# Row sums in tiles of 32 columns, two unused products at the passage to attention, and score banks that lie on those of the projection

## The chip, the core and the metric

The kernel runs on one core of a Trainium2 chip. The core has five engines with instruction streams of their own: TensorE (PE, matrix products; its weight loads are listed as PEld), VectorE (DVE), ScalarE (ACT), GpSimd (POOL) and SyncE (SP, which here issues nearly all DMA transfers). [...] Each engine works through its own stream in order, so an instruction that waits holds up all that stand behind it on that engine. Data lie in SBUF (128 partitions) and in PSUM, where TensorE writes its products: eight banks of 128 partitions by 512 floats.

The metric is device time in microseconds (us). The time before is 2242.26 us, the median of 3 runs (2241.82 to 2245.19).

## The reference, cut to what matters

A transformer block on 2048 tokens of width 576, with all shifts, scales and gates computed from one conditioning row `c`:

```python
mod = (_silu(c) @ w_mod).reshape(1, 6, 1, -1)
sa, ca, ga, sb, cb, gb = (mod[:, i] for i in range(6))
h = _layernorm(x) * (1 + ca) + sa
# attention: 32 heads of width 18, one key head and one value head for all
q, k, v = h @ wq, h @ wk, h @ wv
p = softmax(q k^T * 18**-0.5)
x = x + ga * ((p v) @ wo)
h = _layernorm(x) * (1 + cb) + sb
# channel MLP, hidden width 4608; the layernorm stands inside it once more
x = x + gb * (gelu(_layernorm(h) @ w1 + b1) @ w2 + b2)
```

Everything is in float32. The six rows of `mod` are 576 wide. Rows 0 and 1 are needed at the start; rows 2 to 5 (`ga`, `sb`, `cb`, `gb`) only after attention.

## The kernel before, in words

The program has three stages, and the pool of PSUM tiles is closed and opened again between them (`open_ps`). A new pool hands out banks in the order in which its kinds of tiles are first asked for, and a tile that lies on a bank of the old pool waits for the last users of the old tile there.

**Stage 1** computes the first layernorm and the projections, in four blocks of 512 tokens and five chunks of columns each (`q_chunk`; its product is a tile psB). Here psA has banks 0 to 3 (two tiles of two banks), psC bank 4, psB banks 5 to 7. Already in stage 1 some row maxima of the scores of the first two head groups are computed: `smax_half` (called by `unit`) forms scores in two psA tiles with four products and VectorE reduces each tile (line 337). The last `unit` stands at the end of the last chunk (line 470).

`busy(n)` multiplies the identity with itself n times into a psB tile that nobody reads. It is called three times near the start of the program.

**Stage 2** is attention, in 32 steps called quads (4 heads by 512 tokens). Within a quad the order of the work is written out by hand as a string of tokens (`QUAD`, `QUADW`):

- S: one product of scores, keys by queries, into a psB tile (line 901), and its exponential by ScalarE (line 903) into a tile P. 64 of them in a quad.
- M, R: scores for the row maxima of the *next* quad into a psM tile (line 319), reduced by VectorE (lines 923 and 921). X: an additional difference product for them (line 911) that ScalarE clips (line 914).
- V1 to V4: P times values into psC (line 891), as four products that each write 32 rows of the output and use 32 columns of the array; the digit says how many times 128 columns of P they take. When a quad is through, ScalarE copies psC out (line 715).

S products wait for the maxima of their quad, which come as DMAs of a few rows (line 364). Before, stage 2 asks for psB first (banks 0 to 3), then psM (4 to 6), then psC (7).

After every fourth unit of V, `between` lets a generator, `fill`, take one step: at every odd block of keys. The first filler is `late_weights`. It loads rows 3, 2 and 5 of `w_mod` as tiles of 128 partitions (line 527), multiplies them with silu(c) and adds the five chunks up on GpSimd (`total`, lines 498 and 501). What is left is a sum over the 128 partitions, wanted in every partition: `bcast` multiplies by a 128x128 matrix of ones (`unity`) in two halves of 288 columns (line 521), and VectorE writes the result to its destination (line 522): `BC` for rows 3, 4, 5 and `gab` for row 2. Row 4 follows some steps later in the buffer that row 5 leaves free (line 92), as does `wo` in that of row 2 (line 540); `gab` is then multiplied into `wo` by GpSimd (line 550). These results are first needed several quads later.

**Stage 3** is the MLP, 36 passes over groups of hidden columns, in a Strassen-like form: products of operands `OP` with weights (line 1111), GELU, and a second product into psA (lines 1214 and 1248) which VectorE adds to XT (lines 1220 and 1285). The operands of the second half of the tokens are formed during pass 17 by `form`, from pieces R of `yr`; "=T4" is one subtraction of 128x1024 elements, "+T4" its high part by ScalarE (line 1023), "-T4" its low part (line 1025). `op_pieces(R, e2)` takes the engine for some of them: VectorE for the first half of the tokens, GpSimd for the second.

## Time and profile before

| | |
|---|---|
| median of 3 runs | 2242.26 us |
| the profiled execution, its own time | 2243.08 us |
| its span, first to last instruction | 2241.3 us |
| PE busy | 2212.7 us (99%) |
| DVE busy | 1940.8 us (87%) |
| ACT busy | 1645.1 us (73%) |
| POOL busy | 1524.7 us (68%) |
| mean granted TensorE clock | 0.998 |

In a row of the timeline the first number is the start in us from the start of the span, the second the duration, then engine, line, operation, output and inputs, shapes, how many instructions the row holds, and in square brackets how long the engine was idle before it and what ended that. In a row of stretches there follow, after the length of the stretch, the busy times of PE, PEld, DVE, ACT and POOL with their instructions, the granted TensorE clock, the busy share of the DMA engines, and GB/s. In a row of the chain of waits: start, duration, engine, output tile, line.

### The profile page before, as it was taken

The page shows a single profiled execution, that of the slowest core. Times are in us where ns is not written, and L with a number is a line of the kernel's source. Part 1 is how long each engine was busy: PE and PEld are TensorE (multiplying, and loading weights), DVE is VectorE, ACT ScalarE, POOL GpSimd, SP SyncE. Part 2 cuts the span into 40 slices and gives each one's busy share as a digit, 9 for nine tenths or more (in the row PEclk, how much of TensorE's full clock was granted, in tenths as well). Part 3 has the DMA queues.
Part 4 walks back from the last instruction along what each step waited for, and adds up shares of the span by engine and source line. Part 5 has one row for each costly group of instructions (what it writes and reads, how often), then busy time and mean ns, then how long its engine had stood idle before and what let it go on. Part 6 is the DMA issues. An engine that isn't in the chain of part 4 may idle for free.

```text
span 2241.3 us, 45781 instructions
## 1 busy us (share of the span) xinstructions
PE 2212.7 (99%) x16458; PEld 1442.2 (64%) x16458; DVE 1940.8 (87%) x3420; ACT 1645.1 (73%) x3145; POOL 1524.7 (68%) x1760
## 2 busy tenths in 40 slices
PE   7999999999999999999999999999999999999999
PEld 5644544444444544444444445888888888989898
DVE  7589999999999999999999982887888878888787
ACT  5569999999999999999999997444545544344443
POOL 6654356776877787777776300888888857877776
PEclk9999999999999999999999999999999999999999
DMA  6232034443433333343333101666666646676664
GB/s 229 85 129 75 15 114 138 133 142 110 138 121 126 121 122 115 124 139 115 117 127 127 49 13 48 194 177 179 180 178 176 190 122 181 182 213 191 177 183 125
DMA packets 182404, 303.79 MB, mean 136 GB/s; under 512 B 19243, under 2 KB 74923, under 8 KB 182177
## 3 DMA queue, kind: packets, MB, share of 16 engines
q1 hardware_dynamic: 182033, 300.72, 42.9%
q8 instruction: 130, 2.13, 0.4%
q14 instruction: 97, 0.79, 0.1%
q10 hardware_dynamic: 144, 0.15, 0.0%
HBM read 198.71 MB, written 93.19 MB: 130 GB/s over the span
## 4 chain that ended last, share of the span: by engine, by line
PE 86%; DVE 3%; ACT 3%; POOL 2%; issue 1%; DMA 0%; SPq 0%; POOLq 0%; ACTq 0%
PE psC L891 21%; PE psB L1111 18%; PE psA L1214 16%; PE psB L901 13%; PE psM L319 10%; PE psB L700 2%; ACT P L903 2%; PE psB L911 2%; DVE mx L923 1%; PE psA L1248 1%; PE psA L700 1%; DVE xc L921 0%; PE psB L155 0%; PE psB L357 0%; PE psB L248 0%
## 5 line engine op out<-in xcount | busy, mean ns | idle before, releaser
L903 ACT ACTIVATE P<-psB 128x512 f32<-128x512 f32 x2008 | 1043.8, 619 | 35.0 <-PE psM L319 12.3
L923 DVE TENSOR_REDUCE mx<-psM 128x1 f32<-128x512 f32 x1476 | 938.1, 683 | 37.5 <-PE psM L319 14.9
L319 PE MATMUL psM<-KS,qst 64*128 64x512 f32 x1722 | 601.2, 442 | 0.4 <-DVE mx L923 0.4
L901 PE MATMUL psB<-qst,KS 64*128 64x512 f32 x2008 | 585.1, 429 | 1.7 <-DVE mx L337 1.5
L891 PE MATMUL psC<-P,V 128*32 128x256 f32 (+3 forms) x6424 | 576.3, 448 | 0.5 <-ACT O L715 0.5
L901 PEld LDWEIGHTS psB<-qst,KS 64*128 64x128 f32 x2008 | 303.4, 185 | 218.2 <-ACT P L903 141.3
L1111 PE MATMUL psB<-ops,w1a 128*128 128x512 f32 x1512 | 393.8, 396 | 0.2 <-DVE h L1126 0.2
L319 PEld LDWEIGHTS psM<-KS,qst 64*128 64x128 f32 x1722 | 275.6, 184 | 161.9 <-DVE mx L923 120.4
L1111 PEld LDWEIGHTS psB<-ops,w1a 128*128 128x128 f32 x1512 | 270.1, 188 | 46.6 <-DVE h L1126 0.6
L891 PEld LDWEIGHTS psC<-P,V 128*32 128x32 f32 x6424 | 140.0, 108 | 200.1 <-issue 173.4
L1220 DVE TENSOR_TENSOR XT<-psA,XT 128x576 f32<-128x576 f32 x330 | 241.7, 753 | 19.0 <-PE psA L1214 13.6
L1214 PEld LDWEIGHTS psA<-w2s,big 128*128 128x128 f32 x1584 | 223.0, 188 | 13.9 <-POOL big L1188 2.5
L1214 PE MATMUL psA<-w2s,big 128*128 128x288 f32 x1584 | 230.4, 294 | 0.0
L1124 ACT ACTIVATE psB<-gs 128x512 f32<-128x512 f32 x144 | 86.7, 602 | 130.0 <-DVE gs L1123 130.0
L1188 POOL TENSOR_TENSOR big<-s,big 128x512 fp32r<-128x512 f32 x132 | 170.9, 1295 | 10.6
L1120 ACT ACTIVATE h<-psB,b1t 128x512 f32<-128x512 f32 x144 | 97.9, 680 | 102.5 <-PE psB L1111 81.8
L921 DVE CUSTOM_DVE_ANT_0 xc<-psM,xc 128x512 f32<-128x512 f32 x246 | 165.8, 680 | 3.6 <-PE psB L901 1.5
L914 ACT ACTIVATE xc<-psB 128x512 f32<-128x512 f32 x246 | 152.8, 621 | 8.8 <-PE psM L319 7.4
L735 POOL TENSOR_TENSOR os<-O,os 128x512 fp32r<-128x512 f32 x28 | 36.1, 1289 | 164.8 <-ACT os L734 164.8
L1123 DVE SCALAR_TENSOR_TENSOR gs<-psB,h 128x512 f32<-128x512 f32 x144 | 98.5, 684 | 39.5 <-ACT psB L1121 39.4
L762 POOL TENSOR_TENSOR r<-r,r 128x256 fp32r<-128x256 f32 (+1 forms) x162 | 121.6, 751 | 13.0
L1129 ACT ACTIVATE big<-h 128x512 fp32r<-128x512 f32 x39 | 24.7, 633 | 133.7 <-DVE h L1126 133.7
(214 smaller groups left out, 3341.2 us busy)
## 6 DMA issues: line engine op xcount, KB each, us to landing
w1a<-w1scr SPq DMA_DIRECT2D x252, 256.0 KB
w2s<-w2sum SPq DMA_DIRECT2D x132, 288.0 KB
w1scr<-r SPq DMA_DIRECT2D x126, 256.0 KB
w2s<-w2scr SPq DMA_DIRECT2D x76, 288.0 KB
w2scr<-r SPq DMA_DIRECT2D x72, 288.0 KB
w2sum<-r SPq DMA_DIRECT2D x72, 288.0 KB
qst<-qscr SPq DMA_DIRECT2D x192, 72.0 KB
w1a<-w2scr SPq DMA_DIRECT2D x33, 288.0 KB
```

The source lines that it names most:

```text
L319: pe.matmul(o, QST[n][64 * g:64 * g + 64, p, 128 * qt:128 * (qt + 1)], KS[64 * g:64 * g + 64, 512 * kb:512 * (kb + 1)], start=True, stop=True)
L762: po.tensor_tensor(o[:, n:2 * n], src, o[:, :n].bitcast(F32), op=ALU.subtract)
L891: pe.matmul(PVt[n][32 * j:32 * (j + 1), cs], V[:, kc, :], t[:, j, cs], start=(kc == 0 and h0 == 0), stop=(kc == 15), skip_group_check=True)
L901: pe.matmul(t, KS[64 * g:64 * g + 64, 128 * kc:128 * (kc + 1)], QST[n][64 * g:64 * g + 64, i, :], start=True, stop=True)
L903: ac.activation(P[n, kc][:, 2 * i + g, :], t, AF.Exp, scale=SCALE)
L914: ac.activation(XC[-1], t, AF.Relu)
L921: ve.tensor_tensor_reduce(c, t, c, 1.0, -3.0e38, ALU.add, ALU.max, o)
L923: ve.tensor_reduce(o, t, axis=AX.X, op=ALU.max)
L1111: pe.matmul(o, x, y, start=(first and i == 0), stop=(i == len(terms) - 1), skip_group_check=True)
L1188: po.tensor_tensor(unit(u, 1), x, unit(u, 0).bitcast(F32), op=ALU.subtract)
L1214: pe.matmul(p[:, i, :288], x[:, ts_], W2S[k][:, y], start=(bool(first) and q == 0), stop=(q == 2), skip_group_check=True)
L1220: ve.tensor_tensor(o, p[:, :, :288], o, op=ALU.add)
```

## The change

Four edits:

1. `busy(1)` before and after the last `unit` of stage 1: two products of 128x128 into psB tiles that nobody reads.
2. At the start of stage 2 a psM tile and a psC tile are asked for, and not used. So psM now lies on banks 0 to 2 (psA before), psC on bank 3 (psA), psB on bank 4 (psC of stage 1, long unused) and 5 to 7 (psB of the projection).
3. `bcast` forms the row sum with four products of 32 rows by 144 columns, one in each strip of 32 columns of the array, side by side in one psB tile: strip j holds columns 144j to 144j+143 of the row. VectorE takes the tile out at once as 128x144. Then one partition of each strip is written to a scratch row in DRAM, and from there the row is read into all 128 partitions. Both transfers go through SP's queue, a filler step apart. The first step of each row sum comes one filler step earlier than the whole came before (except for row 4, which starts at the same step); the fillers after `late_weights` come one step later.
4. In `form` only "=T3" stays on VectorE; "=T4" goes to e2, which for the second half of the tokens is GpSimd.

```diff
@@ last chunk of the last block, stage 1
                 if i == 4:
+                    busy(1)
                     unit()
+                    busy(1)
@@ start of stage 2
     open_ps("2", 4)
+    psM(), psC()
@@ late_weights
+    rowscr = [dr.tile([1, D], F32, name="rowscr%d" % n) for n in range(4)]
...
-        def bcast(w, dst, add, scl):
-
-            for h2 in range(2):
-                cs = slice(288 * h2, 288 * (h2 + 1))
-                p = psB()
-                pe.matmul(p[:, :288], unity, w[:, 0, cs], start=True, stop=True)
-                ve.tensor_scalar(dst[:, cs], p[:, :288], scl, add, op0=ALU.mult, op1=ALU.add)
+        def bcast(n, w, dst, add, scl):
+
+            p = psB()
+            for j in range(4):
+                pe.matmul(p[32 * j:32 * (j + 1), :144], unity[:, :32], w[:, 0, 144 * j:144 * (j + 1)], start=True, stop=True,
+                          skip_group_check=True)
+            r = px.tile([128, 144], F32, name="bc", tag="r" + "3543"[n], padded_shape=[128, (256, 256, D, 256)[n]])
+            ve.tensor_scalar(r, p[:, :144], scl, add, op0=ALU.mult, op1=ALU.add)
+            sy.dma_start(rowscr[n].rearrange("o (j c) -> (o j) c", j=4), r.rearrange("(j p) c -> j p c", p=32)[:, 0, :])
+            yield
+            sy.dma_start(dst, rowscr[n].to_broadcast([128, D]))
             yield
...
-            if i > 5 and i % 2:
+            if i > 5:
                 next(rows)
@@ op_pieces
-                    (e2 if w == "=T1" else ve).tensor_tensor(o, x, y, op=ALU.subtract)
+                    (ve if w == "=T3" else e2).tensor_tensor(o, x, y, op=ALU.subtract)
```

Three places show how instructions move. Line numbers of the changed kernel are 9 higher from line 600 on.

TensorE at the passage from stage 1 to stage 2, with the semaphores that an instruction waits for. L248 is the last projection, L319 into psA the last `unit`, L901 the first S, L319 into psM the first M. Before:

```order
L248 MATMUL psB<-big,wA 126x512 x4
L319 MATMUL psA<-KS,qst 128x512 [waits DVE_49] x2
L319 MATMUL psA<-KS,qst 128x512 x2
L901 MATMUL psB<-qst,KS 128x512 [waits DMAHW5_49,DMAHW4_49,DVE_49]
L319 MATMUL psM<-KS,qst 128x512
L901 MATMUL psB<-qst,KS 128x512 [waits DMAHW7_49,DMAHW6_49,DVE_49]
L901 MATMUL psB<-qst,KS 128x512
L319 MATMUL psM<-KS,qst 128x512 [waits Activation_49]
```

and with the change (L394 is `busy`, L910 the S product):

```order
L248 MATMUL psB<-big,wA 126x512 x4
L394 MATMUL psB<-ident 128x128 [waits Activation_49]
L319 MATMUL psA<-KS,qst 128x512 [waits DVE_49] x2
L319 MATMUL psA<-KS,qst 128x512 x2
L394 MATMUL psB<-ident 128x128
L910 MATMUL psB<-qst,KS 128x512 [waits DMAHW5_49,DMAHW4_49]
L319 MATMUL psM<-KS,qst 128x512 [waits DVE_49]
L910 MATMUL psB<-qst,KS 128x512 [waits DMAHW7_49,DMAHW6_49,Activation_49]
```

A product now stands ahead of the last `unit` and one behind it; the first S no longer waits for VectorE, and the first M does.

SP's queue from the loads of `w_mod` to the maxima of the third quad (L364); L315 loads queries, L92 is row 4 of `w_mod`. Before:

```order
L527 DMA bigw<-in_wmod 128x5x576 x3
L364 DMA qst<-ms 1x8x128 x4
L315 DMA qst<-qscr 18x2x512 x6
L92 DMA bigw<-in_wmod 128x5x576
L540 DMA bigw<-in_wo 128x5x576
L364 DMA qst<-ms 1x8x128 x4
```

and with the change:

```order
L536 DMA bigw<-in_wmod 128x5x576 x3
L364 DMA qst<-ms 1x8x128 x4
L529 DMA rowscr_1281<-bc 4x144
L315 DMA qst<-qscr 18x2x512 x6
L531 DMA BC<-rowscr_1281 128x576
L529 DMA rowscr_1282<-bc 4x144
L531 DMA gab<-rowscr_1282 128x576
L529 DMA rowscr_1283<-bc 4x144
L531 DMA BC<-rowscr_1283 128x576
L92 DMA bigw<-in_wmod 128x5x576
L549 DMA bigw<-in_wo 128x5x576
L364 DMA qst<-ms 1x8x128 x4
```

Six small transfers now stand ahead of the load of row 4 and of the maxima of the third quad; two more stand ahead of the maxima of the fourth.

VectorE in pass 17 of stage 3, where "=T4" (L1016) stood between a GELU step (L1126) and two additions of psA to XT (L1285). Before:

```order
L1285 TENSOR_TENSOR XT<-psA,XT 128x576
L1123 SCALAR_TENSOR_TENSOR gs<-psB,h 128x512
L1389 TENSOR_TENSOR psB<-psB,u 128x512
L1126 SCALAR_TENSOR_TENSOR h<-psB,h 128x512
L1016 TENSOR_TENSOR yr<-yr 128x1024
L1285 TENSOR_TENSOR XT<-psA,XT 128x576 x2
```

and GpSimd in the same pass with the change, where the first L1025 row is the subtraction that came over and the second is "=T1", which was there:

```order
L1034 TENSOR_TENSOR ops<-yr,ops 128x1024
L1141 TENSOR_TENSOR big<-h,big 128x512
L1025 TENSOR_TENSOR yr<-yr 128x1024
L1141 TENSOR_TENSOR big<-h,big 128x512
L1025 TENSOR_TENSOR yr<-yr 128x1024
```

It stands between two low parts of GELU results (L1141) on GpSimd, and on VectorE the two additions follow the GELU step at once.

More of the change, by code (lines that the diff above doesn't have):

```diff
@@ L529, in late_weights @@
         sums = (x for t in (m5, m2, m3) for x in total(t))
-        rows = (x for a in ((m5, BC[:, 2, :], 0.0, 0.5), (m2, gab, 0.0, 1.0), (m3, BC[:, 0, :], 0.0, 1.0))
+        rows = (x for a in ((0, m5, BC[:, 2, :], 0.0, 0.5), (1, m2, gab, 0.0, 1.0), (2, m3, BC[:, 0, :], 0.0, 1.0))
                 for x in bcast(*a))
@@ L545, in late_weights @@
         yield
-        yield from bcast(m4, BC[:, 1, :], 1.0, 1.0)
+        yield from bcast(3, m4, BC[:, 1, :], 1.0, 1.0)
         wos = pw.tile([128, 2, KD, D], F32R, name="wos", tag="wA", padded_shape=[128, 2, KD, WQC])
```

## The prediction

> **What bounds the kernel now.** First the page: busy shares, then the chain that ended last.

> ```profile
> PE 2212.7 (99%) x16458; PEld 1442.2 (64%) x16458; DVE 1940.8 (87%) x3420; ACT 1645.1 (73%) x3145; POOL 1524.7 (68%) x1760
> PE 86%; DVE 3%; ACT 3%; POOL 2%; issue 1%; DMA 0%; SPq 0%; POOLq 0%; ACTq 0%
> ```

> TensorE is the bound almost everywhere, so an edit pays only where it shortens TensorE's stream, fills its gaps, or keeps its clock up. I looked at the three places that the edits touch, by stretches.

> The row sums first. The products of the first, then three stretches, each from one copy of psC (ScalarE, line 715) to the next, so each one quad long:

> ```profile
> 173.09 1.24 PE L521 MATMUL psB<-bigw,unity 128*128 128x288 f32 x4
> 173.39:214.60 41.21, 41.21 (x375) 20.26 (x375) 39.55 (x77) 37.32 (x77) 11.06 (x9) 1.00 0.31 100
> 214.60:253.32 38.72, 38.72 (x367) 19.21 (x366) 37.65 (x73) 37.08 (x76) 18.51 (x16) 1.00 0.05 12
> 253.32:290.70 37.38, 37.38 (x363) 18.55 (x362) 36.55 (x71) 36.96 (x76) 11.58 (x11) 1.00 0.16 46
> ```

> The third has no row sum, the second one, the first three (one of them begun before it): the quads grow by 1.34 us and 3.83 us. So a row sum now costs its full price. ScalarE, 36.96 of 37.38 us busy in a quad without one, is nearly a second bound.

> Now the passage to attention. First the stretches, cut so that the drop of the clock begins at a border, then the timeline:

> ```profile
> 124.63:128.05 3.42, 2.60 (x12) 1.15 (x8) 2.51 (x3) 1.09 (x2) 0.70 (x1) 1.00 0.47 156
> 128.05:131.46 3.41, 1.92 (x10) 0.99 (x9) 3.15 (x4) 1.22 (x3) 0.57 (x1) 1.00 0.52 146
> 131.46:134.87 3.41, 3.06 (x13) 1.96 (x12) 3.41 (x7) 3.40 (x7) 0.00 (x0) 0.50 0.76 197
> 134.87:138.29 3.42, 3.42 (x17) 1.03 (x14) 1.28 (x3) 1.91 (x5) 0.00 (x0) 0.50 1.04 383
> 15.41:18.82 3.41, 2.07 (x21) 1.90 (x20) 2.33 (x5) 1.62 (x6) 1.75 (x4) 1.00 1.06 374
> 18.82:22.23 3.41, 3.41 (x17) 3.07 (x17) 2.90 (x5) 2.77 (x5) 1.65 (x3) 0.50 1.05 390
> 46.13:49.54 3.41, 2.43 (x11) 1.54 (x11) 1.31 (x2) 3.02 (x5) 2.95 (x6) 1.00 0.46 144
> ...
> 127.89 2.36 DVE L337 TENSOR_REDUCE mx<-psA 128x2 f32<-128x1024 f32 x2 [0.59 <-PE psA L319]
> 129.17 0.50 PE L901 MATMUL psB<-qst,KS 64*128 64x512 f32 x1 [1.09 <-DVE mx L337]
> ```

> After a window of 3.41 us in which TensorE was busy for 1.92 us (56%) its granted clock is 0.50 for two such windows. The same happens once near the start, after 2.07 us (61%). After 2.43 us (71%) and 2.60 us (76%) it stayed at 1.00. So somewhere between 61% and 71% a window decides. The hole is S waiting for the last reductions of stage 1, whose psA banks its psB lies on.

> Last, pass 17 of stage 3:

> ```profile
> 1804.59 1.29 POOL L1132 TENSOR_TENSOR big<-h,big 128x512 fp32r<-128x512 f32 x1
> 1804.66 2.31 DVE L1016 TENSOR_TENSOR yr<-yr 128x1024 f32<-128x1024 f32 x1 [0.81 <-POOL ops L1025]
> 1806.89 1.41 DVE L1285 TENSOR_TENSOR XT<-psA,XT 128x576 f32<-128x576 f32 x2
> 1807.69 0.43 PEld L1248 LDWEIGHTS psA<-w2s,big 128*128 128x128 f32 x3 [1.69 <-DVE XT L1285]
> 1807.69 0.66 PE L1248 MATMUL psA<-w2s,big 128*128 128x288 f32 x3 [1.26 <-DVE XT L1285]
> ...
> 1811.00 1.68 POOL L1132 TENSOR_TENSOR big<-h,big 128x512 fp32r<-128x512 f32 x1 [5.12 <-ACT big L1129]
> ```

> The subtraction (line 1016) holds VectorE for 2.31 us; the additions that free psA come late, and TensorE stands still for 1.26 us.

> **The change part by part.** *Row sums.* The nearest rows for the new form are V products, which also use strips of 32 columns; then one row sum as it stands now, from the chain of waits:

> ```profile
> 183.31 0.57 PE psC L891 x8
> 183.88 1.17 PE psB L521 x4
> 185.04 0.35 PE psC L891 x8
> ...
> 177.20 1.06 PE L891 MATMUL psC<-P,V 128*32 128x512 f32 x8
> 184.97 0.42 PE L891 MATMUL psC<-P,V 128*32 128x128 f32 x8
> ```

> Four strips of 256 columns take 0.57 us of the chain, of 128 columns 0.35, so 0.22 per 128 columns and 0.13 to begin with. Four of 144 columns: 0.35 + 16/128 x 0.22 = 0.38 us. Now: 3.83 in the first quad, 0.30 of the first sum that lies ahead of it (173.09 to 173.39, where its products begin), 1.34 in the second: 5.47 us for four. Then 4 x 0.38 = 1.52. The term is -3.95 us. If the 0.20 by which a quad grows beyond the 1.17 of the products (a change of form in the array) stays too, 3.15 are won; if ScalarE's pace hides the new products, all 5.47. VectorE is relieved as well (one piece of 144 columns for two of 288). Eight transfers are added; what they can delay on SP:

> ```profile
> 174.69 0.60 SPq L92 DMA_DIRECT2D bigw<-in_wmod  x1
> 203.94 2.85 SPq L364 DMA_DIRECT2D qst<-ms  x4
> 205.74 4.17 POOL L498 TENSOR_TENSOR bigw<-bigw,st 128x1152 f32<-128x1152 f32 x2
> 166.17 5.67 POOL L501 TENSOR_TENSOR bigw<-bigw 128x1152 f32<-128x1152 f32 x3
> 233.59 1.24 PE L521 MATMUL psB<-bigw,unity 128*128 128x288 f32 x4
> ```

> The load of row 4 now stands behind the third sum's transfers. The first two sums stand 10.8 us apart (173.09, 183.88), which is two filler steps; so the third was at about 195 and now, a step earlier, comes at about 189. The load goes out at about 190 instead of 174.69; 1.47 MB at the 383 GB/s of the stretch from 134.87 take 4 us. GpSimd uses it at 205.74, the next maxima go out at 203.94; both are clear by then. GpSimd has the third total at 171.84 (166.17 + 5.67), well ahead of the earlier third sum. I cost the transfers at nothing; without that cover, each us late would be one of TensorE's.

> *The passage.* The two products are each a 128-column float32 product; one stands ahead of products that wait for VectorE, the other in the hole of 1.09 us that ends at 129.17, so their own cost is nothing. The first S no longer waits for VectorE: TensorE is free from 128.08 (129.17 less the 1.09), so behind the product it can go at about 128.4; its exponential comes earlier by as much. The first M must now wait for the reduction that ends at 129.07, where it stood at 129.28 anyway. The maxima keep VectorE busy back to back, so nothing is won directly before 134. What can be won is the clock. The window from 128.05 had 1.92 us; a product of 0.27 us (below) and 0.50 of the S brought forward make 2.69 us, 79%. The borders need not lie there in each execution: were the window 127.0 to 130.4, it holds 3.41 less some 1.8 of waiting, plus the same 0.77, about 70%: at the edge.

> ```profile
> 122.81 0.27 PE L357 MATMUL psB<-ident,mxf 128*16 128x128 f32 x1
> 131.10 4.28 DVE L923 TENSOR_REDUCE mx<-psM 128x1 f32<-128x512 f32 x7 [0.26 <-PE psB L901]
> 134.10 1.88 DVE L923 TENSOR_REDUCE mx<-psM 128x1 f32<-128x512 f32 x3
> 135.39 1.93 PE L891 MATMUL psC<-P,V 128*32 128x512 f32 x8
> ```

> If the clock stays up: 6.83 us at half speed hold 3.4 us of loss at most, if TensorE alone set the pace. Up to about 134.2 VectorE does, with a reduction each 0.61 us (4.28/7). From there to 138.29 TensorE does: the V of 512 columns takes 1.93 for 1.06 us, and VectorE and ScalarE go idle. Half of 4.1 us: -2.0 us, bounds 0 and -3.4.

> *The subtraction.* Without it the additions can start where it started, at 1804.66, not at 1806.89; TensorE's 1.26 us vanish. On GpSimd it follows line 1132 at about 1805.9 and ends near 1808.3, in a hole of 5.12 us; nothing behind it there runs before 1811.00. Without that hole it would put off the low part of a GELU result by its length. The term is -1.26 us, bounds -0.9 (the additions 0.4 us slower beside GpSimd, an estimate from its 1.68 for 1.29 us beside VectorE) and -1.7 (the weight loads' wait).

> *The banks at the passage to stage 3.* One psA tile there now lies partly on psC:

> ```profile
> 1387.41 6.64 PE L700 MATMUL psA<-wos,big 126*128 126x288 f32 x48
> 1387.58 0.60 ACT L715 ACTIVATE O<-psC 128x512 f32<-128x512 f32 x1 [1.20 <-PE psC L891]
> ```

> It is the second 24 of these 48 products, from about 1390.7; psC is out at 1388.2. Nothing.

> Sum: -3.95 - 2.0 - 1.26 = -7.2 us. Against the profiled execution's own 2243.08 us that is 2235.9; this execution lies 0.8 above the median of 2242.26, so a median of **2235.0 us**.

> **The rivals.** *A: the clock drops all the same.* For it: 70% in an unlucky window lies inside the band of 61 to 71%, and if the DMAs of maxima hold the first S until 129.17, the window has only 1.92 + 0.27 = 2.19 us, 64%. Then the second term is nothing: -5.2 us, 2237.0. Against it: in the window as profiled 79% is above all that dropped. [...]

> *B: the strips run one after another.* Then four times 144/128 x 0.22 and the start make 1.1 us each, where 1.37 stood: -1.0 for four, in sum -1.0 - 2.0 - 1.26 = -4.3 us, 2238.0: not told from no change. Against it: a V of 512 columns would take 4 x 0.88 us, not 1.06.

> *C: SP's queue.* If a transfer of a row sum held SP until row 4 lands late, the fourth sum (products at 233.59 now) would stand in TensorE's stream and wait, and such a hole would drop the clock too. GpSimd needs some 11 us for the total (4.17 for four of the five chunks, the fifth, 5.67 for the additions), so row 4 must come after 222 for the first loss; after 234 it eats the gains of 7.2, and at 239 or later the time is 2247 or more. It comes at about 195, so the slack is some 27 us; a transfer of 4 rows would have to hang for that long.

> **How the numbers follow.** Forecast 62%, A 25%, B 7%, C 6% (with the unnamed). The range takes the bounds: all gains at their largest 5.47 + 3.4 + 1.7 = 10.6 us, 2231.7; with A and small gains 3.15 + 0.9 = 4.1, 2238.2. I set 2231.5 to 2239.5. A change under 0.2% (4.5 us) can't be told from none. Faster: nearly all of the forecast and seven tenths of A, 0.78; same 0.16, the rest of these and B; slower 0.06, C.

> **What would show it.** Row sums: x8 in 0.38 us of the chain, the two quads at 39 and 37.8 us. The passage: granted clock 1.00 from 128 to 140, the V of 512 columns at 1.06. Pass 17: no wait of line 1248 for VectorE. I am wrong if 0.50 shows there again, if the quads with sums stay over 38 and 40 us, or if a row sum waits for GpSimd or a DMA.

## The result, and the profile after

| | before | changed |
|---|---|---|
| median | 2242.09 us (2240.18 to 2245.31, 10 runs) | 2236.81 us (2235.77 to 2237.54, 10 runs) |
| profiled execution, its own time | 2243.08 us | 2236.47 us |
| its span | 2241.3 us | 2234.7 us |

The ratio is 0.9977, with an interval of 0.9969 to 0.9985: 5.28 us less. That is faster (the interval leaves out 1; it means 3.4 to 7.0 us less), inside the range, 1.8 us above the forecast and within 0.2 us of rival A, the forecast without its clock term.

Where the 6.61 us between the two profiled executions went, by the times at which the same instruction stands in both (copies of the maxima, copies of psC, additions to XT):

| stretch | changed less before |
|---|---|
| to the first copy of maxima, 123 us, ahead of every edit | -0.74 |
| the passage, from there to the second copy of maxima | -0.66 |
| from there to the third copy of psC: the four row sums | -3.63 |
| from there to pass 17 of stage 3 | within 0.1 |
| pass 17, with the subtraction | -1.60 |

The first row is no effect of the change. The row sums and the subtraction make 3.63 + 1.60 = 5.23 us, close to the 5.28 of the medians; their interval leaves room for the 0.66 of the passage as well.

The busy times of the changed kernel's page, and its shares of the chain of waits:

```profile
PE 2211.4 (99%) x16478; PEld 1443.2 (65%) x16478; DVE 1935.6 (87%) x3415; ACT 1645.8 (74%) x3145; POOL 1529.3 (68%) x1761
PE 88%; DVE 3%; ACT 3%; issue 1%; POOL 0%; ACTq 0%; POOLq 0%; DVEq 0%
```

TensorE has 20 instructions more (a float32 product counts as two here: 16 more for the row sums, 4 for the two single products) and is still the bound. GpSimd has left the chain: 2% of it before, 0% now.

**Row sums.** The three stretches from one copy of psC to the next, columns as in the view of before:

```profile
172.63:210.48 37.85, 37.85 (x379) 18.94 (x378) 37.02 (x73) 37.08 (x77) 11.11 (x9) 1.00 0.40 133
210.48:248.29 37.81, 37.81 (x371) 18.79 (x370) 36.78 (x72) 37.05 (x76) 14.99 (x13) 1.00 0.08 20
248.29:285.68 37.39, 37.39 (x363) 18.50 (x362) 36.58 (x71) 36.97 (x76) 15.17 (x15) 1.00 0.14 42
```

41.21, 38.72 and 37.38 us have become 37.85, 37.81 and 37.39: the quad without a row sum is unmoved, and two sums cost 0.46 where they and a part of a third cost 3.83. The first and the last sum in the chain of waits (start, duration, engine, tile and line, how many instructions):

```profile
167.19 0.29 PE psB L525 x8
167.48 0.03 DVEq L528
167.51 0.42 DVE mx L932
167.93 0.23 DVE bc L528
168.16 0.04 issue
168.20 0.49 PE psB L910
...
228.72 0.78 PE psC L900 x8
229.50 0.24 PE psB L525 x8
229.75 0.43 PE psB L910
```

A sum is 0.24 to 0.29 us of the chain instead of 1.17. The first one also makes the next S wait: its psB tile comes free only when VectorE, behind a reduction, has taken the sum out (0.42 + 0.23 us). At the last there is no such wait.

**The passage.** In this trace the granted clock changes at 13.14, 19.96, 26.79, 129.19 and 136.02 us; the steps between are 2, 2, 30 and 2 times 3.413 us. A stretch of that length on these borders is called a window here. Three windows at the passage, then five rows of the timeline:

```profile
125.78:129.19 3.41, 2.53 (x10) 1.21 (x9) 2.81 (x3) 1.38 (x4) 1.28 (x1) 1.00 0.26 88
129.19:132.60 3.41, 3.15 (x12) 1.66 (x11) 3.12 (x6) 2.69 (x5) 0.00 (x0) 0.50 0.70 216
132.60:136.02 3.42, 3.42 (x16) 1.33 (x16) 2.67 (x5) 3.27 (x7) 0.00 (x0) 0.50 0.98 309
```

```profile
127.28 0.49 PE L394 MATMUL psB<-ident 128*128 128x128 f32 x2
127.70 0.50 PE L910 MATMUL psB<-qst,KS 64*128 64x512 f32 x1
128.45 0.50 PE L319 MATMUL psM<-KS,qst 64*128 64x512 f32 x1 [0.24 <-DVE mx L337]
134.68 1.70 PE L900 MATMUL psC<-P,V 128*32 128x512 f32 x8
137.21 1.07 PE L900 MATMUL psC<-P,V 128*32 128x512 f32 x8
```

The edit does what it says: the first S (L910) goes 0.75 us before the first M (L319), which waits for VectorE in its place. But the clock stands at 0.50 for two windows again, though TensorE was busy for 2.53 of the 3.41 us ahead of them. The V of 512 columns takes 1.70 us there and 1.07 as soon as the clock is back.

**Pass 17.** The three engines around the subtraction, which is now the first L1025. The first row has the two additions that stood behind it on VectorE before, the fourth the products that waited for them:

```profile
1798.77 1.60 DVE L1294 TENSOR_TENSOR XT<-psA,XT 128x576 f32<-128x576 f32 x2
1799.59 1.30 POOL L1141 TENSOR_TENSOR big<-h,big 128x512 fp32r<-128x512 f32 x1
1800.86 2.39 POOL L1025 TENSOR_TENSOR yr<-yr 128x1024 f32<-128x1024 f32 x1
1801.28 0.57 PE L1257 MATMUL psA<-w2s,big 128*128 128x288 f32 x3
1803.09 0.76 DVE L1294 TENSOR_TENSOR XT<-psA,XT 128x576 f32<-128x576 f32 x1 [0.32 <-PE psA L1257]
1803.51 1.28 POOL L1141 TENSOR_TENSOR big<-h,big 128x512 fp32r<-128x512 f32 x1 [0.26 <-ACT big L1138]
```

These products no longer wait; the next addition waits for TensorE instead (0.32 us). The next low part on GpSimd waits for ScalarE, not for the subtraction ahead of it.

### The profile page after: what moved, and what is told of

Its sections match the earlier page's. It is cut to its first block, busy times and chain, and to the rows that moved or that the text cites. A ratio compares the mean times of both kernels' runs of the same rounds, so it can differ in the third digit from the quotient of the medians.

```text
span 2234.7 us, 45830 instructions
## 1 busy us (share of the span) xinstructions
PE 2211.4 (99%) x16478; PEld 1443.2 (65%) x16478; DVE 1935.6 (87%) x3415; ACT 1645.8 (74%) x3145; POOL 1529.3 (68%) x1761
## 4 chain that ended last, share of the span: by engine, by line
PE 88%; DVE 3%; ACT 3%; issue 1%; POOL 0%; ACTq 0%; POOLq 0%; DVEq 0%
PE psC L900 22%; PE psB L1120 18%; PE psA L1223 16%; PE psB L910 13%; PE psM L319 11%; PE psB L709 2%; ACT P L912 2%; PE psB L920 2%; PE psA L1257 1%; DVE mx L932 1%; PE psA L709 1%; DVE xc L930 0%; PE psB L155 0%; PE psB L357 0%; PE psB L248 0%
## 5 line engine op out<-in xcount | busy, mean ns | idle before, releaser
L319 PE MATMUL psM<-KS,qst 64*128 64x512 f32 x1722 | 601.3, 442 | 0.5 <-DVE mx L337 0.5
L910 PE MATMUL psB<-qst,KS 64*128 64x512 f32 x2008 | 585.4, 429 | 0.3 <-ACT P L912 0.2
L910 PEld LDWEIGHTS psB<-qst,KS 64*128 64x128 f32 x2008 | 303.6, 185 | 215.6 <-ACT P L912 140.8
L319 PEld LDWEIGHTS psM<-KS,qst 64*128 64x128 f32 x1722 | 275.8, 184 | 163.7 <-DVE mx L932 121.7
L1197 POOL TENSOR_TENSOR big<-s,big 128x512 fp32r<-128x512 f32 x132 | 171.0, 1296 | 10.6
L1129 ACT ACTIVATE h<-psB,b1t 128x512 f32<-128x512 f32 x144 | 98.1, 681 | 102.2 <-PE psB L1120 81.4
L923 ACT ACTIVATE xc<-psB 128x512 f32<-128x512 f32 x246 | 152.5, 620 | 7.1 <-PE psM L319 5.6
L1132 DVE SCALAR_TENSOR_TENSOR gs<-psB,h 128x512 f32<-128x512 f32 x144 | 98.5, 684 | 40.0 <-ACT psB L1130 39.9
```

The costliest lines, as they stand in the source:

```text
L319: pe.matmul(o, QST[n][64 * g:64 * g + 64, p, 128 * qt:128 * (qt + 1)], KS[64 * g:64 * g + 64, 512 * kb:512 * (kb + 1)], start=True, stop=True)
L910: pe.matmul(t, KS[64 * g:64 * g + 64, 128 * kc:128 * (kc + 1)], QST[n][64 * g:64 * g + 64, i, :], start=True, stop=True)
L923: ac.activation(XC[-1], t, AF.Relu)
L1197: po.tensor_tensor(unit(u, 1), x, unit(u, 0).bitcast(F32), op=ALU.subtract)
```

## The experiments

Besides time and ratio to the kernel before, each is read by the length of its first quad, from the first copy of maxima to the second, against the same stretch of before: that leaves out what the clock did in stage 1. The changed kernel has -0.66 us there.

### Each edit alone

**e1_sums**: the kernel before with the new row sums alone.

```diff
...
+            for j in range(4):
+                pe.matmul(p[32 * j:32 * (j + 1), :144], unity[:, :32], w[:, 0, 144 * j:144 * (j + 1)], ...
...
```

> The kernel before with the new row sums alone (strips of 32 columns, the row by way of DRAM). Theory: a row sum costs about 0.4 us of TensorE's stream instead of 1.3, so the two quads that followed the first copy of psC shrink from 41.2 and 38.7 us to 37.9 and 37.8, and the time falls by 3.5 to 4 us, to about 2238.3; the wait in pass 17 and the first quad stay as before. Rival (strips one after another): about 1 us in all, the quads stay over 38 and 40 us.

2239.07 us (2237.97 to 2242.48), ratio 0.9989 (0.9980 to 0.9999). From the second copy of maxima to the third copy of psC it is 3.60 us shorter than before, as the changed kernel is by 3.63; the passage is as before (-0.07). This execution began 2.91 us late, for a reason ahead of the edit:

```profile
45.46:48.87 3.41, 1.27 (x10) 0.98 (x9) 1.85 (x7) 1.65 (x3) 2.98 (x6) 1.00 0.23 79
48.87:52.28 3.41, 3.41 (x11) 2.03 (x9) 1.98 (x2) 3.35 (x7) 1.55 (x3) 0.50 0.78 250
```

The first of these windows, in stage 1, holds only 1.27 us of TensorE's work, and a further window at half clock follows. So marks within one execution say more of an edit here than its time.

**e2_passage**: the kernel before with the two single products and the moved banks alone.

```diff
+                    busy(1)
                     unit()
+                    busy(1)
...
+    psM(), psC()
```

> The kernel before with the two unused products and the moved banks alone. Theory after the result (rival A): the granted clock drops to 0.50 for two windows at the passage all the same, and only the earlier S and the place of the drop can matter: 0 to 0.7 us. The forecast's first idea: the clock stays at 1.00 and 2 us are won. The quads with row sums stay at 41.2 and 38.7 us, the wait in pass 17 stays.

2242.18 us (2240.80 to 2247.04), ratio 1.0003 (0.9994 to 1.0012): nothing. First quad -0.30.

```profile
127.54:130.95 3.41, 2.93 (x14) 1.43 (x11) 3.24 (x4) 1.75 (x4) 0.89 (x1) 1.00 0.45 125
130.95:134.36 3.41, 3.34 (x12) 1.94 (x12) 3.41 (x7) 3.12 (x6) 0.00 (x0) 0.50 0.72 202
134.36:137.78 3.42, 3.42 (x16) 1.05 (x15) 1.29 (x3) 1.91 (x5) 0.00 (x0) 0.50 1.03 391
```

TensorE was busy for 86% of the window ahead (2.93 of 3.41), and the clock fell all the same. A bound of 61 to 71% by busy time can't be what decides.

**e3_sub**: the kernel before with the moved subtraction alone.

```diff
-                    (e2 if w == "=T1" else ve).tensor_tensor(o, x, y, op=ALU.subtract)
+                    (ve if w == "=T3" else e2).tensor_tensor(o, x, y, op=ALU.subtract)
```

> The kernel before with the subtraction of 128x1024 elements in pass 17 moved to GpSimd alone. Theory: TensorE's wait for VectorE in pass 17 goes, and the passes from 18 on start 1.3 to 1.7 us earlier; all else as before: about 2240.6. Rival: GpSimd delays a low part of a GELU result, a wait of the second product for GpSimd takes the place, and nothing is won.

2240.87 us (2239.70 to 2242.30), ratio 0.9991 (0.9982 to 1.0001). The additions to XT run 0.82 us late up to pass 17 (the passage, with three windows at half clock, took 0.61 more) and 0.78 us early behind it: the edit gives 1.60 us, as in the changed kernel.

The three ratios make -2.5, +0.7 and -2.0 us, together -3.8 where the changed kernel has -5.28; their intervals are some 2 us to each side, so this is no contradiction. The marks are sharper: 3.60, 0.30 and 1.60.

### Does the strip form run side by side?

**e8_sum4**: the changed kernel with each row sum's four products issued four times (the same values are written four times).

```diff
-            for j in range(4):
+            for j in 4 * (0, 1, 2, 3):
```

> The changed kernel with the four products of each row sum issued four times over (the same results, written again). Theory (four strips run side by side): 12 more products of 144 columns cost 3 x 0.24 = 0.7 us per row sum, 2.9 us in all; the two quads after the first copy of psC grow from 37.85 and 37.81 us to about 39.4 (two sums lie in it) and 38.5. Rival (one after another): 3 x 0.96 = 2.9 us per sum, 11.5 in all, the quads at 43.6 and 40.7.

A single run: 2241.47 us, 2 us of it from a window at half clock in stage 1. The quad with two sums grows by 1.47 us, that with one by 0.57, the stretch ahead of both, with one, by 0.44: 2.48 us for four sums, 0.62 for each twelve products, 0.21 for four. The first sum's row in the chain of waits, and all instructions of the line (shortest, median and longest in ns):

```profile
169.71 0.98 PE psB L525 x32
```

```profile
L525 PE MATMUL psB<-bigw,unity x128: 286/286/286, 169.5 to 234.7; 128*32 128x144 f32 x128
```

One instruction lasts 0.29 us; four products, eight instructions, cost 0.21. They run side by side, and rival B falls.

### What holds the clock at the passage

**e4_fill**: the changed kernel with three products ahead of the last `unit` and five behind it, and one full 128x128 product after each M of the first steps.

```diff
-                    busy(1)
+                    busy(3)
                     unit()
-                    busy(1)
+                    busy(5)
...
+                if n == 0 and pq <= LAG:
+                    fillup(1)
```

> The changed kernel with TensorE filled up at the passage: three unused products instead of one before the last unit, five instead of one behind it, and one unused product of 128x128 (into psC, which no one uses yet) after each maximum product of the first quad until the first V. Results are the same. Theory (idle TensorE drops the clock): the granted clock stays at 1.00 from 125 to 140, the first V of 512 columns takes about 1.06 us, and the time falls by 1 to 2 us against the changed kernel, to about 2235. Rival (the drop has another cause, or products of 64 rows do not count): 0.50 for two windows shows again and the time is that of the changed kernel or up to 1 us more.

2240.55 us (2239.57 to 2243.21), ratio 0.9994 (0.9985 to 1.0004). The clock stays at 1.00 and the V of 512 columns takes 1.06 us; yet the first quad is 3.22 us longer than before. The chain of waits there (L492 is the inserted product):

```profile
131.51 0.42 PE psC L492 x2
131.92 0.42 PE psB L916
132.35 0.01 PE psM L319
132.36 0.42 PE psC L492 x2
132.77 0.42 PE psM L319
```

An inserted product takes 0.42 us of the chain (two instructions), and the S or M behind it 0.42 too. The changed kernel's chain shows what an S or M costs behind its like:

```profile
169.49 0.43 PE psB L910
169.91 0.23 PE psM L319 x2
170.14 0.23 PE psB L910 x2
```

Only the first of a run, behind the V, costs 0.43; of those that follow, each two add 0.23. The filler keeps the clock and loses more than the clock is worth: its ten products make the first quad 5.3 us longer than that of e5, below, which has none.

**e5_busy8** and **e11_busy8_again**: only the eight products around the `unit`, without a filler; **e10_behind5**: one ahead and five behind.

```diff
-                    busy(1)
+                    busy(3)
                     unit()
-                    busy(1)
+                    busy(5)
```

> The changed kernel with three unused products instead of one before the last unit of stage 1 and five instead of one behind it; nothing in the first quad. In the run with TensorE filled up, these eight cost nothing that the trace shows (first maximum reduced at the same point); the ones inside the first quad cost 0.42 us each and more. Theory (only products inside the first quad hold the clock, since there TensorE waits for VectorE with half of the array's rows in use): 0.50 shows again for two windows, time as the changed kernel within 0.5 us. Rival (the hole before the first S alone sets the drop): 1.00 throughout, first V of 512 columns at 1.06 us, about 1 us won.

> [...] Theory: the clock holds at the passage again, and the first quad is again 1.4 us shorter than in the changed kernel; time 2234.5 to 2236. Rival (luck of the window): 0.50 for two windows, first quad as in the changed kernel, time 2236.8.

> One unused product before the last unit as in the changed kernel, five behind it. Theory (the hole of 1.09 us behind the unit decides): the clock holds, 2235.2. Rival (the holes before and within the unit count as much): 0.50 again, 2236.8.

e5: 2235.20 us (2234.19 to 2235.32), ratio 0.9967 (0.9954 to 0.9980). e11, the same kernel: 2235.44 (2234.61 to 2237.49), 0.9972 (0.9961 to 0.9982). e10: 2236.01 (2234.97 to 2237.81), 0.9974 (0.9965 to 0.9983). The clock stays at 1.00 through the passage in all three, and their first quads are 2.07, 2.09 and 2.09 us shorter than before. Two rows of e5:

```profile
126.49 1.38 PE L394 MATMUL psB<-ident 128*128 128x128 f32 x10
133.11 1.06 PE L900 MATMUL psC<-P,V 128*32 128x512 f32 x8
```

And three windows of e10 on its own clock's borders:

```profile
121.99:125.40 3.41, 3.41 (x17) 2.18 (x16) 1.36 (x4) 1.11 (x3) 1.28 (x1) 1.00 0.08 28
125.40:128.82 3.42, 2.78 (x16) 1.86 (x16) 2.83 (x3) 1.09 (x2) 1.27 (x1) 1.00 0.40 131
128.82:132.23 3.41, 2.88 (x17) 1.52 (x15) 3.41 (x6) 2.48 (x6) 0.00 (x0) 1.00 0.66 196
```

After 2.78 and 2.88 us of busy time the clock stays at 1.00 here; after 2.93 in e2 it fell. The five products behind the `unit` suffice here; the two more ahead of it are not told apart. All runs agree, profiled or not: over all runs of a kernel the mean granted clock is 0.9986 to 0.9992 for every kernel with five or more products behind the `unit`, and 0.9970 to 0.9976 for those whose profiles show the drop (e8, with its single run, apart).

**e6_fill64**: e5, with one product of 64 rows, the form of S, after each M of the first steps.

```diff
...
+        pe.matmul(spare, KS[:64, :128], QST[0][:64, 0, :], start=True, stop=True)
...
```

> As the run before, and with one unused product of the form of S (64 rows, 512 columns, into psC, which nobody uses yet) after each maximum product of the first quad until the first V. Theory: without the change of form it costs at most 0.21 us each and lies beside VectorE's 0.61 us per reduction, so the 3.2 us that the full-array products cost do not come. If products of 64 rows count for the clock, it stays at 1.00 and the first quad is 1 us shorter than in the changed kernel (about 2235.8); if they do not, 0.50 shows again and the time is that of the changed kernel or up to 1 us more.

2236.07 us (2235.01 to 2238.17), ratio 0.9971 (0.9960 to 0.9982). The clock holds, and the first quad is 1.25 us shorter than before: the filler costs 0.8 us against e5. In the form of its neighbours it is much cheaper than e4's, but nothing is left for it to win.

**e9_nobanks8**: e5 without `psM(), psC()`, so with the banks of before.

```diff
-    psM(), psC()
```

> Eight unused products, but the banks of the kernel before. Theory (the hole before the first S is what counts, and the products fill it whatever comes behind): the clock holds as well, and the moved banks are worth nothing beside them: time within 0.5 us of the version with moved banks, 2235.2. Rival (the S that the moved banks let through early belong to it): 0.50 again, about 1.4 us more.

2235.76 us (2234.38 to 2238.78), ratio 0.9972 (0.9961 to 0.9983). The clock holds, first quad -1.83: the moved banks are worth about 0.25 us there, too little for the ratios to show.

**e7_nobusy**: the changed kernel without the two products; **e12_after_again**: the changed kernel as it is, beside e11.

```diff
-                    busy(1)
                     unit()
-                    busy(1)
```

> The changed kernel without the two unused products; the banks stay moved. Theory: the clock drops at the passage with them and without them, so they are worth nothing: the time is that of the changed kernel (2236.8) within what can be measured, and the first quad as long within 0.7 us. Rival: they shorten the drop by a window or shift it; then it is three windows long here and the first quad 0.6 us longer.

> The changed kernel once more, for a second profile beside the version with eight products on the same chip. Theory (two products are too few in every place of the window): 0.50 for two windows again, 2236 to 2237.5. Rival: 1.00 here, so that two products suffice in some executions.

e7: 2237.79 us (2235.20 to 2239.46), ratio 0.9980 (0.9971 to 0.9989); two windows at half clock, first quad -0.35. e12: 2237.31 (2235.44 to 2239.97), 0.9979 (0.9969 to 0.9988); two windows again, first quad -0.44. The two products alone change nothing that can be told.

**The windows counted another way.** Busy time doesn't sort the windows, so for each I counted columns from its trace: an instruction of TensorE counts its columns times the share of the array's 128 rows that it uses (a half for S and M), spread evenly over its recorded time. The emptiest window at the passage:

| kernel | window | busy, us | columns | clock of the next |
|---|---|---|---|---|
| e12 | 125.73 to 129.14 | 2.51 | 2054 | 0.50 |
| changed | 125.78 to 129.19 | 2.53 | 2074 | 0.50 |
| e1 | 130.79 to 134.20 | 1.92 | 2224 | 0.50 |
| before | 128.05 to 131.46 | 1.92 | 2300 | 0.50 |
| e3 | 125.56 to 128.97 | 1.91 | 2323 | 0.50 |
| e7 | 127.41 to 130.83 | 2.53 | 2558 | 0.50 |
| e8 | 129.35 to 132.76 | 2.84 | 2559 | 0.50 |
| e2 | 127.54 to 130.95 | 2.93 | 2768 | 0.50 |
| e4 | 133.68 to 137.09 | 3.41 | 2553 | 1.00 |
| e10 | 125.40 to 128.82 | 2.78 | 2993 | 1.00 |
| e9 | 128.77 to 132.19 | 2.82 | 3262 | 1.00 |
| e11 | 130.50 to 133.92 | 2.95 | 3388 | 1.00 |
| e5 | 127.07 to 130.49 | 2.99 | 3552 | 1.00 |
| e6 | 126.65 to 130.06 | 3.19 | 3781 | 1.00 |

The eight that fell hold 2,768 or fewer, and of the six that held all but e4's (2,553) hold 2,993 or more. Over the whole of these fourteen profiles, 23 windows at full clock are followed by one at half clock; all hold 2,768 columns or fewer, and of the 9,050 others only four do. Without the share of rows the columns sort far worse: 99 windows that held then lie below the fullest that fell. In this count `busy(1)` adds 256 and `busy(5)` 1,280: 1,024 more would lift the changed kernel's window from 2,074 to 3,098. The count was found in these same traces and was not tried on a kernel made for it, so it is a reading that fits and not a thing shown.

## Why the prediction was right, and where it was wrong

*Row sums, -3.95 forecast, -3.60 to -3.63 measured* (e1, e7, the changed kernel). The mechanism holds: the full price was paid before, four strips run side by side (e8), and SP's part is hidden, and so is VectorE's, except at the first sum. The price of 0.38 us was too high for the products, 0.24 to 0.29 in the chain. What makes the term smaller than forecast is a wait that the sum had left out: psB of the first sum is held until VectorE has taken it out, 0.65 us of the chain. The second quad came as forecast (37.8 us). The first came at 37.85, not 39: all of the first sum now lies ahead of it, and 39 is also more than three sums of 0.38 add to 37.38 (38.5).

*SP's queue, nothing forecast.* Nothing came of it. The load of row 4 went out at 190.90, about where it was put; the changed kernel is 5.03 us ahead at the third copy of psC, behind all transfers of the row sums, and 5.00 at pass 17. Rival C has no row that speaks for it.

*The clock, -2.0 forecast, nothing measured.* This is the step that failed: "somewhere between 61% and 71% a window decides". The window did fill, to 74%, between the 79% and the 70% worked out for two placings of it, and the clock fell; with 86% in e2 it fell too. The first quad is 0.12 to 0.66 us shorter than before in e2, e7, e8, e12 and the changed kernel, all with moved banks, with the clock down in all of them. That the clock fell made rival A's number right, though not by A's reason: A had an unlucky window inside the band or the first S held by a transfer. Neither was there: the S went at 127.70, and the window lay above the band. The price was about right where the clock was held: e5, e10 and e11 are 2.07 to 2.09 us shorter in the first quad than before, and e9, with the banks of before, 1.83. Against the changed kernel's two profiles, in which the clock fell, they are 1.4 to 1.7 us shorter.

*Gaps and busy time.* The longest gap of TensorE does not sort the windows either: it is 1.09 us in that of before, 0.63 in the changed kernel's and 0.25 in e2's, and the clock fell after all three, while it held in e10 after a gap of 0.64. In before, too, the clock changes in steps of 3.413 us: its two falls, at 18.82 and 131.46, lie 112.64 us apart, 33 of them. That TensorE's busy time in the window ahead decides was my estimate, and no run shows it. If the count above holds, busy time was the wrong stand-in: a product of 64 rows weighs half there, though in before an instruction of 512 columns is busy for 0.39 us (median) with 64 rows, in S, as with 128, in the projection.

*The subtraction, -1.26 forecast, -1.60 measured.* Right mechanism, wrong row: the wait of the weight loads (1.69 us), given as the bound, comes nearer than the products' 1.26. Both waits end at 1807.69; that of the weight loads begins 0.43 us earlier. The products stand 1.41 us earlier right behind the wait and 1.60 from 1811 on. That a stall is priced by the weight loads fits this one place and was not tried elsewhere. GpSimd had room, as forecast.

*The sum.* -3.63 - 1.60 = -5.23 lies close to the measured -5.28. The subtraction came out 0.34 larger and the row sums 0.32 smaller than forecast, and the clock's 2.0 is missing. That two misses cancel is luck, and so is how close rival A's number came; the time lies in the range, for all that the clock's term failed, because the range reached up to rival A with small gains.

## What to carry to other kernels

Where the profile shows half clock behind a thin stretch, put enough full products into its hole: here five behind the `unit` hold the clock and are worth 1.4 to 1.7 us against the changed kernel's two profiles and 2.1 against before, while one on each side is worth nothing that can be told. The kernel with eight has the lowest medians of all (2235.20 and 2235.44 us), though its intervals overlap with the changed kernel's. In a stream of another form full products cost some 0.5 us apiece (5.3 us for ten). When a stall of TensorE is priced, look at the idle time of its weight loads as well as that of its products: here 1.60 us came back, against 1.69 and 1.26.
